# Fetching the K cache in 4 MB units of 32 pairs by 512 keys, with dense score tiles, in a decode attention and MLP kernel

## The chip, the cores and the metric

The kernel runs on one core of a Trainium2 chip, the other cores idle. The metric is the device time of one execution in microseconds (us). A profile is one execution taken with the hardware profiler. Its span (first to last instruction) is about 1.3 us shorter than the measured time.

Engines: PE is TensorE (PEld its weight loads), DVE is VectorE, ACT is ScalarE, POOL is GpSimd, SP is SyncE, whose queue here issues nearly all transfers.

## The reference

The output mixes sliding-window decode attention and a GELU MLP. There are 8 batches, 32 query heads, 16 kv heads of 128, a window of the last 2048 of 8192 keys, and a model width of 576.

```python
g = sigmoid((x * gate_w).sum(-1))
q = (x @ wq).reshape(8, 1, 32, 128)
k, v = last 2048 keys of k_cache, v_cache          # each 8 x 16 pairs of (2048, 128) bf16
p = softmax(q k^T / sqrt(128));  a = (p v) @ wo
b = gelu(layernorm(x) @ w1 + b1) @ w2 + b2
out = g * a + (1 - g) * b
```

The windows of K and V are 67 MB each, the weights 20 MB. Each byte of K and V is used for two query heads only, so this is a memory-bound job. A "pair" below is one batch with one kv head: 512 KB of K in the window, and 2 MiB of the cache, because the cache holds 8192 keys.

## The kernel before

The kernel lists its operations, orders them for each engine when it is built, and emits them with semaphores. Nine slots of 2 MB are shared by K, V and weights, in a ring. K is fetched in 32 units of 2 MB, each 4 batches of one kv head, with each of 128 partitions receiving one contiguous run of 64 keys (16 KB).

```python
def src_of(cache, g, q):
    hkv, b0 = 2 * g + q // 2, 4 * (q % 2)
    return cache[b0:b0 + 4, hkv, S0:Sk, :].rearrange("a (x r) d -> x a (r d)", x=32)

def take_slot():
    n = n_slot[0]; n_slot[0] += 1
    return (n + 6) % NSLOT            # NSLOT = 9, one ring for K, V and weights

def k_unit(i):                        # 32 of them; four make a group g, then softmax(g)
    d = dma("sp", ... slot(s), src_of(A_k_cache, g, q) ..., deps=slot_free[s])
    for h in range(2):
        tr = add("dve", transpose 128x2048 f32 words of the slot -> KT[n % 2], deps=[d, qk_half[n - 2]])
        # first of a group: 4 mask matmuls put -1e9 where query and key belong to different pairs
        # then 8 matmuls, 128 weight columns each (weights held for four), into four PSUM banks
        # PSUM rows: 32 groups' queries x 2048 keys, mostly masked
    slot_free[s] = trs                # the slot goes back after both transposes

def softmax(g):                       # 8 of them
    mx = DVE max over ps[:, 0:4, :]   # 128 x 2048
    ...                               # maximum over the four quadrants, negated and scaled
    for c in range(4): ACT exp of 512 columns, with sum
    for c in range(4): DVE transpose of 512 columns of P -> PT[g % 2]
```

A V unit (2 MB) is multiplied by PT as it lies: 16 matmuls, an eviction by ACT, and 8 small float32 matmuls that add it up. Then the wo projection is added as soon as its head is ready. The order of transfers is K0 to K4, then K and V by turns with four wo chunks between, then b2 and the four w2 chunks, the last of them cut in three.

## Time and profile before

| | before |
|---|---|
| time | 367.79 us (3 runs, 367.7 to 367.86) |
| bytes read | 154.31 MB, 421 GB/s over the span |
| DVE busy, PE busy, ACT busy | 211, 257, 48 us |
| K and V packets | 8192 of 16 KB, 611 ns each |
| tail from the last w2 packet to the end | 2.8 us |

The next lines are from the page of the kernel before. First comes busy time by engine, then the span in 40 slices (busy tenths and GB/s), the bytes, and the shares of the chain that ended last.

```profile
span 366.4 us, 3881 instructions
PE 257.0 (70%) x1815; PEld 86.4 (24%) x1429; DVE 210.7 (57%) x258; ACT 47.8 (13%) x117; POOL 24.3 (7%) x67
DMA  9999999999999999999999999999999999999995
GB/s 378 442 398 427 427 435 432 431 427 431 431 429 429 420 428 427 431 430 433 427 438 431 406 439 429 429 435 427 431 429 429 416 435 435 426 431 433 408 428 224
HBM read 154.31 MB, written 0.01 MB: 421 GB/s over the span
DMA 61%; DVE 17%; PE 16%; SPq 4%; issue 1%; ACT 0%; DVEq 0%
```

The DMA engines are full from the first slice to the last but one, at about 430 GB/s. The chain of waits gives only 61% to DMA, and the rest to DVE and PE. Those pieces are true waits (a slot is handed back by a transpose), but they run beside full DMA engines.

The next lines are groups of instructions before: line, engine, operation, shapes and count, busy time and mean ns, then idle time before it and what ended it. They are the K transpose, the maximum, the exponential and the transpose of P.

```profile
L644 DVE STREAM_TRANSPOSE arena<-arena 128x2048 f32<-128x2048 f32 x64 | 145.4, 2298 | 77.1 <-DMA arena<-in_A_k_cache_dram 64.9
L590 DVE TENSOR_REDUCE arena<-ps 128x1 f32<-128x2048 f32 x8 | 18.3, 2282 | 14.9 <-PE ps L175 14.9
L604 ACT ACTIVATE arena<-ps,arena 128x512 bf16<-128x512 f32 x32 | 21.6, 686 | 39.7 <-DVE arena L599 39.7
L609 DVE STREAM_TRANSPOSE arena<-arena 128x512 bf16<-128x512 bf16 x32 | 19.9, 674 | 0.8 <-ACT arena L604 0.8
```

### The profile page before, as it was taken

The page shows a single profiled execution, that of the slowest core. Times are in us where ns is not written, and L with a number is a line of the kernel's source. Part 1 is how long each engine was busy: PE and PEld are TensorE (multiplying, and loading weights), DVE is VectorE, ACT ScalarE, POOL GpSimd, SP SyncE. Part 2 cuts the span into 40 slices and gives each one's busy share as a digit, 9 for nine tenths or more (in the row PEclk, how much of TensorE's full clock was granted, in tenths as well). Part 3 has the DMA queues.
Part 4 walks back from the last instruction along what each step waited for, and adds up shares of the span by engine and source line. Part 5 has one row for each costly group of instructions (what it writes and reads, how often), then busy time and mean ns, then how long its engine had stood idle before and what let it go on. Part 6 is the DMA issues. An engine that isn't in the chain of part 4 may idle for free.

```text
span 366.4 us, 3881 instructions
## 1 busy us (share of the span) xinstructions
PE 257.0 (70%) x1815; PEld 86.4 (24%) x1429; DVE 210.7 (57%) x258; ACT 47.8 (13%) x117; POOL 24.3 (7%) x67
## 2 busy tenths in 40 slices
PE   0269882896699398664967397765957397865885
PEld 0259200131122032010311032011311032114542
DVE  0704699798667754479544764478544864473000
ACT  1010002101300300013100300003100300003200
POOL 7010000000001000000000000000000000000000
PEclk9999998799689879696988879696988879695659
DMA  9999999999999999999999999999999999999995
GB/s 378 442 398 427 427 435 432 431 427 431 431 429 429 420 428 427 431 430 433 427 438 431 406 439 429 429 435 427 431 429 429 416 435 435 426 431 433 408 428 224
DMA packets 14922, 154.58 MB, mean 422 GB/s; under 512 B 1292, under 2 KB 5556, under 8 KB 6072
## 3 DMA queue, kind: packets, MB, share of 16 engines
q1 hardware_dynamic: 14848, 154.29, 99.2%
q8 instruction: 13, 0.21, 0.2%
q10 hardware_dynamic: 56, 0.03, 0.0%
q14 instruction: 5, 0.04, 0.0%
HBM read 154.31 MB, written 0.01 MB: 421 GB/s over the span
## 4 chain that ended last, share of the span: by engine, by line
DMA 61%; DVE 17%; PE 16%; SPq 4%; issue 1%; ACT 0%; DVEq 0%
DMA arena<-in_A_k_cache_dram 50%; DVE arena L644 12%; DMA arena<-in_B_w_dram 11%; PE ps L175 7%; DVE arena L590 2%; PE ps L501 2%; PE ps L661 2%; PE ps L684 2%; SPq L630 2%; PE ps L699 2%; SPq L677 1%; DVE arena L609 1%; SPq L749 1%; PE ps L503 1%; DVE arena L599 0%
## 5 line engine op out<-in xcount | busy, mean ns | idle before, releaser
L644 DVE STREAM_TRANSPOSE arena<-arena 128x2048 f32<-128x2048 f32 x64 | 145.4, 2298 | 77.1 <-DMA arena<-in_A_k_cache_dram 64.9
L175 PE MATMUL ps<-arena 128*128 128x512 bf16 x401 | 138.1, 456 | 14.7 <-DVE arena L644 9.3
L661 PE MATMUL ps<-arena 128*128 128x512 bf16 x115 | 52.4, 456 | 15.0 <-DVE arena L644 14.9
L693 ACT ACTIVATE arena<-ps 128x512 f32<-128x512 f32 x32 | 19.1, 598 | 198.0 <-PE ps L684 198.0
L661 PEld LDWEIGHTS ps<-arena 128*128 128x128 bf16 x128 | 15.0, 117 | 124.9 <-issue 69.2
L699 PE MATMUL ps<-arena 128*128 128x8 f32 x256 | 35.2, 269 | 8.7 <-ACT arena L693 7.7
L684 PE MATMUL ps<-arena 128*32 128x512 bf16 x512 | 35.6, 403 | 6.7 <-DMA arena<-in_A_v_cache_dram 6.6
L699 PEld LDWEIGHTS ps<-arena 128*128 128x128 f32 x256 | 34.0, 208 | 21.7 <-ACT arena L693 16.8
L653 PE MATMUL ps<-arena 128*128 128x512 bf16 x6 | 3.5, 585 | 36.9 <-DVE arena L609 36.9
L590 DVE TENSOR_REDUCE arena<-ps 128x1 f32<-128x2048 f32 x8 | 18.3, 2282 | 14.9 <-PE ps L175 14.9
L604 ACT ACTIVATE arena<-ps,arena 128x512 bf16<-128x512 f32 x32 | 21.6, 686 | 39.7 <-DVE arena L599 39.7
L637 POOL TENSOR_TENSOR arena<-arena 128x128 bf16<-128x128 bf16 x32 | 12.7, 401 | 165.0 <-PE ps L175 156.2
L684 PEld LDWEIGHTS ps<-arena 128*32 128x32 bf16 x512 | 11.2, 99 | 40.8 <-issue 24.0
L609 DVE STREAM_TRANSPOSE arena<-arena 128x512 bf16<-128x512 bf16 x32 | 19.9, 674 | 0.8 <-ACT arena L604 0.8
L544 PE MATMUL ps<-arena 128*8 128x288 bf16 (+1 forms) x140 | 12.5, 333 | 2.4 <-DMA arena<-in_B_w_dram 2.3
L717 POOL TENSOR_TENSOR arena<-arena 128x16 bf16<-128x16 f32 x15 | 4.0, 267 | 146.3 <-ACT arena L709 146.3
L501 PE MATMUL ps<-arena 128*128 128x8 bf16 x144 | 10.9, 201 | 3.1 <-DMA arena<-in_B_w_dram 3.1
L501 PEld LDWEIGHTS ps<-arena 128*128 128x128 bf16 x144 | 10.8, 158 | 3.6 <-DMA arena<-in_B_w_dram 3.6
L653 PEld LDWEIGHTS ps<-arena 128*128 128x128 bf16 x8 | 0.9, 107 | 44.1 <-DVE arena L609 44.1
L717 DVE TENSOR_TENSOR arena<-ps,arena 128x16 bf16<-128x16 f32 x1 | 0.2, 229 | 18.1 <-PE ps L699 18.1
L423 PE MATMUL ps<-arena 8*128 8x8 bf16 x8 | 0.6, 171 | 13.9 <-DVE arena L396 10.3
L616 DVE RECIPROCAL arena<-ps 128x32 f32<-128x32 f32 x8 | 2.9, 358 | 11.9 <-PE ps L614 11.9
(85 smaller groups left out, 96.3 us busy)
## 6 DMA issues: line engine op xcount, KB each, us to landing
arena<-in_A_k_cache_dram SPq DMA_DIRECT2D x32, 2048.0 KB, 33.7
arena<-in_A_v_cache_dram SPq DMA_DIRECT2D x32, 2048.0 KB, 34.8
arena<-in_B_w_dram SPq DMA_DIRECT2D x1, 4608.0 KB, 23.9
arena<-in_A_wo_dram SPq DMA_DIRECT2D x4, 1152.0 KB, 37.6
arena<-in_A_wq_dram SPq DMA_DIRECT2D x1, 4096.0 KB, 13.6
arena<-in_B_w_dram SPq DMA_DIRECT2D x3, 1296.0 KB, 14.7
arena<-in_B_w_dram SPq DMA_DIRECT2D x3, 576.0 KB, 16.1
arena<-in_A_wq_dram SPq DMA_DIRECT2D x1, 512.0 KB, 4.0
```

The costliest lines, as they stand in the source:

```text
L175: return e.add_instruction(mybir.InstMatmult(name=nc.get_next_instruction_name(), engine=mybir.EngineType.PE, ins=[e.lower_ap(rhs), e.lowe ...
L501: ins = e.matmul(out_, lhsT, yT[:, kt, :], start=(kt == 0), stop=False)
L544: ins = e.matmul(ps[32 * j:32 * j + 8, BK_ACC, 0:JN], lhsT, rhs[:, JN * j:JN * j + JN], start=False, stop=True, skip_group_check=True, til ...
L590: mx = add("dve", lambda e: e.tensor_reduce(out=k(MX), in_=ps[:, 0:4, :].rearrange("p a n -> p (a n)"), axis=AXL.X, op=ALU.max), deps=[qk_ ...
L604: return e.activation(out=Pm[:, 512 * c:512 * c + 512], in_=ps[:, c, :], func=ACTF.Exp, bias=k(NB), scale=SCALE, accum_out=k(SUM + c))
L609: pts.append(add("dve", (lambda c=c: lambda e: e.transpose(bass.AP(arena, offset=aoffs("PT") + 2048 * (g % 2) + 128 * c, ap=[[AST, 128], [ ...
L637: return e.tensor_tensor(out=dst, in0=src, in1=own, op=ALU.mult)
L644: tr = add("dve", (lambda h=h, kb=kb: lambda e: e.transpose(bass.AP(arena_f, offset=foffs("KT") + kb * 2048, ap=[[AST // 2, 128], [1, 2048]]),
L661: mm = e.matmul(*args, start=False, stop=last) if rc == 0 else held_matmul(nc, e, *args, stop=last)
L684: mm = e.matmul(ps[c:c + 32, BK_OS[i % 2], :], PT[:, g % 2, 512 * q + 32 * t:512 * q + 32 * t + 32], slot(s)[:, 512 * t:512 * t + 512], st ...
L693: u_ev[i] = add("act", lambda e: e.activation(out=EV[:, i % 2, :], in_=ps[:, BK_OS[i % 2], :], func=ACTF.Copy), deps=[prev] + ([u_sum[i - ...
L699: mm = e.matmul(ps[:, BK_S, OC + 16 * (item % 2) + 8 * (q % 2):OC + 16 * (item % 2) + 8 * (q % 2) + 8], EV[:, i % 2, 128 * r:128 * r + 128 ...
```

## The change

The intent is to read K in longer runs and to stop computing scores that are thrown away.

- **Transfers.** A K unit becomes 4 MB: 32 neighbouring pairs by 512 keys, and each partition gets a run of 128 keys (32 KB). K has two 4 MB buffers of its own; V has five 2 MB slots.
- **Scores.** Each matmul has 32 weight columns and writes 32 of the 128 PSUM rows, one row block for each K unit of a group, so a bank holds 128 x 512 scores that are all wanted. The mask matmuls go. A softmax now covers one bank: a maximum over 512 columns in place of 2048, and one exponential in place of four. Two softmaxes follow every fourth K unit.
- **Layout of P.** V's matmuls still want the old layout. So the dense tile is copied four times, each time masked to one of four query groups, and transposed from there with a stride.
- **V units.** Still 2 MB and 16 KB runs, but the four pairs of a unit are now eight pairs apart; before, they were one kv head of four batches.
- **End.** A kv head's output is complete only when all four groups are done, so the whole wo projection moves to the end, and so do the wo transfers.

The core of the diff, with cuts:

```diff
+        order = ("0 1 v 2 v 3 v 4 v v 5 v v 6 v v 7 v v 8 v v 9 v v 10 v v 11 v v 12 v v 13 v v 14 v 15 "
+                 "w w v v w w v v v v v v")          # numbers: K units; then b2 and the w2 chunks
         def take_slot():
-            return (n + 6) % NSLOT
+            return 4 + n % 5
         def k_unit(i):
-            d = dma("sp", lambda e: e.dma_start(slot(s), src_of(A_k_cache, g, q)), ...)
+            G, c = divmod(i, 4)
+            s = 2 * (i % 2)
+            src = bass.AP(A_k_cache.tensor, offset=(32 * G * Sk + S0 + 512 * c) * Dh, ap=[[Sk * Dh, 32], [128 * Dh, 4], [1, 128 * Dh]])
+            d = dma("sp", ... RAW[:, s * SE:(s + 2) * SE], src ..., deps=slot_free[s] + slot_free[s + 1])
...  # 8 matmuls for each half and bank:
+            mm = e.matmul(ps[32 * c:32 * c + 32, 2 * (G % 2) + nb, :], qb[:, G % 2, n, 2 * h + ee, :], rhs, ..., tile_position=(0, 32 * c))
         def softmax(g):
-            mx = ... in_=ps[:, 0:4, :] ...
+            mx = ... in_=ps[:, bank, :] ...
-            for c in range(4): activation(out=Pm[:, 512 * c:512 * c + 512], in_=ps[:, c, :], func=ACTF.Exp, ...)
+            ex = activation(out=view("Pd"), in_=ps[:, bank, :], func=ACTF.Exp, ...)
+            for a in range(4): tensor_scalar(out=P[a], in0=Pd, scalar1=amask[:, a:a + 1], op0=ALU.mult)
...
+        def project():                        # called after the last V, before b2
+            for n in range(8):
+                for hkv in (n, n + 8):
+                    AccGroup("proj%d" % hkv, mms, [oT_done[n + 8 * m] for m in range(4)] + [d], cost=0.5)
```

## The prediction

> **What bounds the kernel now.** The transfers. The page shows DMA as 9 in 39 of 40 slices; queue 1 alone takes 99.2% of 16 engines' span, 154.3 MB. In the records of all DMA packets at least 16 are in flight all the time, except for about 2 us at the start and 3.5 us at the end. In the table by stretches every stage from 25 to 345 us runs at 429 to 432 GB/s, while DVE is busy 53 to 76% of a stage and PE 70 to 82%. The chain of waits is 61% DMA; its DVE and PE pieces lie beside full DMA. So compute time saved is worth nothing by itself. The Trainium skill ("DMA: Bandwidth & Descriptors", section "Where 436 GB/s comes from") gives 435 GB/s as the ceiling of the ports; the 431 seen here agrees.
>
> **What the change does to the transfers.** Same bytes. K goes from 16 KB runs to 32 KB runs. In the packet records a 16,384-byte packet takes 611 ns and a 32,768-byte one (wq, median) 1213 ns: 4.5 ns less per 16 KB. K has 4096 such packets, 256 per engine: 1.15 us saved. That is all there is to gain.
>
> **What it does to compute (estimates from the trace's durations).**
> - DVE: 64 K transposes (2.30 us each) become 32 of twice the size, about 4.45 us: 147 to 142 us. The maximum over 2048 columns (8 x 2.28) becomes one over 512 (about 0.65): -13 us. Masked copies: 32 x 0.2 to 0.3: +8 us. The transposes of P (0.67 us) now read with a stride of 512 bytes: 0.7 to 1.4 us: 0 to +22 us. Total 205 to 225 us (211 before), under 62% of the span.
> - ACT: 32 exponentials become 8: -16 us, to about 31 us.
> - PE: 512 score matmuls stay, 32 mask matmuls go; each score matmul loads its own 32-column weights. I expect 0.22 to 0.33 us each, PE 210 to 260 us busy.
>
> None is near the transfer time.
>
> **What moves.** K gets two 4 MB buffers, V five 2 MB slots; before, nine slots were shared. Per 8 MB (K, V, V: 19.5 us at 431 GB/s) DVE has 9 us of transposes, plus some 18 us of softmax each fourth time. A K buffer is handed back 9 to 11 us after landing and needed 25 us or more after. Two places are tight, with 1 to 3 us to spare: K2 at the start (only K1 and one V lie between it and K0, and DVE does the GELU at 38 to 41 us), and the third wo chunk at the end, which waits for the last K's transposes. A stall there costs 0 to 3 us.
>
> **Risk.** The 16 DMA engines now read K side by side at a 2 MiB pitch (one pair each), before at 16 KB. The same page (section "Latency and other measured facts", row "HBM row pitch at large powers of two") reports lower rates at such pitches. No record of this trace shows that pattern, so a fall of the K rate is my main way to lose more than 2%.
>
> **Prediction.** 367.3 us, range 365.6 to 371.5. Faster by over 2%: 0.02; within 2%: 0.87; slower by over 2%: 0.11.
>
> **What would show it.** Right: DMA 9 in nearly all slices at about 430 GB/s; 2048 packets of 32 KB at about 1213 ns; K issues waiting long for DVE without any dip in GB/s; ACT near 31 us. Wrong: 32 KB packets of 1300 ns or more (pitch), GB/s dips at 45 to 55 us or near 310 us (buffers too few), K transposes far above 4.5 us (DVE then becomes the bound), or a tail after the last w2 transfer longer than the 2 to 3 us of before.

## More of the kernel before

The next lines are DMA issues before: out and in, count, KB each, and median us from issue to landing.

```profile
arena<-in_A_k_cache_dram SPq DMA_DIRECT2D x32, 2048.0 KB, 33.7
arena<-in_A_v_cache_dram SPq DMA_DIRECT2D x32, 2048.0 KB, 34.8
```

A transfer of 2 MB moves in 4.9 us at 430 GB/s, so 34 us from issue to landing means that about seven transfers stand in the queue. This is the stock that keeps DMA full while compute is uneven.

The next lines are the end of the kernel before, in order of time on PE: start, duration, instruction, and in brackets the idle time before it and who ended it.

```profile
353.03 6.38 PE L544 MATMUL ps<-arena 128*8 128x288 bf16 x56
360.95 2.03 PE L544 MATMUL ps<-arena 128*8 128x288 bf16 x26 [1.54 <-DMA arena<-in_B_w_dram]
363.71 0.78 PE L544 MATMUL ps<-arena 128*8 128x288 bf16 x10 [0.73 <-DMA arena<-in_B_w_dram]
```

PE waits for w2 twice (1.54 and 0.73 us), so the end is set by the transfer.

## The result

| | before | after |
|---|---|---|
| time, median | 367.83 us (4 runs, 367.7 to 367.97) | 367.9 us (4 runs, 367.75 to 367.98) |
| ratio after / before | | 1.0002, 95% interval 0.9984 to 1.0019 |
| packet time per DMA engine (sum over 16) | 364.66 us | 363.57 us |
| last w2 packet ends at | 363.7 us of 366.4 | 363.1 us of 366.6 |
| tail from there to the end | 2.8 us | 3.5 us |
| DVE, PE, ACT busy | 211, 257, 48 us | 211, 257, 31 us |

Here and below a ratio is the one for the fast runs of both kernels, with its 95% interval; it is not quite the ratio of the medians. The packet rows come from adding up the DMA packet records of the two traces.

These are the same lines of the page after.

```profile
span 366.6 us, 4165 instructions
PE 256.9 (70%) x1805; PEld 131.4 (36%) x1805; DVE 210.9 (58%) x255; ACT 31.0 (8%) x69; POOL 17.5 (5%) x80
DMA  9999999999999999999999999999999999999994
GB/s 374 441 419 431 420 436 445 413 451 402 458 411 442 422 434 434 425 452 406 451 413 447 420 442 422 438 421 434 426 445 422 438 388 440 403 431 431 430 420 187
HBM read 154.31 MB, written 0.01 MB: 421 GB/s over the span
DMA 41%; PE 28%; DVE 28%; issue 1%; SPq 1%; ACT 1%; DVEq 0%
```

DMA is full again, with the same bytes and the same rate. The chain of waits looks quite different (DMA 41% in place of 61%), at the same time to 0.1%. That warns against reading its shares as costs.

These are the groups after: K transpose, maximum, exponential, masked copies and transpose of P.

```profile
L652 DVE STREAM_TRANSPOSE arena<-arena 128x4096 f32<-128x4096 f32 x32 | 141.1, 4432 | 85.3 <-DMA arena<-in_A_k_cache_dram 80.7
L586 DVE TENSOR_REDUCE arena<-ps 128x1 f32<-128x512 f32 x8 | 5.5, 692 | 13.5 <-PE ps L664 13.4
L597 ACT ACTIVATE arena<-ps,arena 128x512 bf16<-128x512 f32 x8 | 5.5, 687 | 115.3 <-DVE arena L595 115.3
L604 DVE TENSOR_SCALAR arena<-arena 128x512 bf16<-128x512 bf16 x32 | 9.0, 345 | 1.0 <-ACT arena L597 0.8
L612 DVE STREAM_TRANSPOSE arena<-arena 128x512 bf16<-128x512 bf16 x32 | 30.6, 1016 | 0.0
```

DVE saves 4 us of K transposes and 13 us of maxima. It pays 9 us for masked copies and 11 us more for the transposes of P. The sum is the same.

The transposes of P now read single 2-byte elements 512 bytes apart, and take 1016 ns in place of 674. The Trainium skill ("SBUF — State Buffer", section "Door 1: The DMA port swizzle") says that SBUF has 16-byte lines and that accesses which cross to a new line pay. The larger duration agrees with that; no run here isolates the stride.

These are the DMA issues after.

```profile
arena<-in_A_k_cache_dram SPq DMA_DIRECT2D x16, 4096.0 KB, 24.9
arena<-in_A_v_cache_dram SPq DMA_DIRECT2D x32, 2048.0 KB, 23.6
```

A transfer now lands 24 us after its issue, not 34. At the same rate this means that less is queued. The time does not show this loss.

This is the end of the kernel after, on PE:

```profile
353.86 1.06 PE L710 MATMUL ps<-arena 128*128 128x8 f32 x8 [0.47 <-ACT arena L704]
357.33 1.06 PE L710 MATMUL ps<-arena 128*128 128x8 f32 x8 [0.46 <-ACT arena L704]
358.31 6.34 PE L544 MATMUL ps<-arena 128*8 128x288 bf16 x96
```

There is no wait for a transfer any more. PE works through 96 projection and w2 matmuls without a gap up to 364.7 us. The w2 data came earlier than before, but PE was behind.

So the trace gives this account of the time. The longer runs save 1.08 us of packet time. The last packet ends 0.5 us earlier. The tail is 0.7 us longer. The last two sum to about zero.

The step from 1.08 to 0.5 us can be read from the same records. Packets that follow each other on an engine overlap a little: the time with more than 16 packets in flight on the main queue, averaged over the 16 engines, adds up to 3.4 us before and 2.8 us after. The sum of packet times counts the overlap twice, so only about 0.5 us of the 1.08 is a shorter transfer.

### The profile page after: what moved, and what is told of

It reads as the page before. It is cut to its first block, busy times and chain, and to the rows that moved or that the text cites. A ratio compares the mean times of both kernels' runs of the same rounds, so it can differ in the third digit from the quotient of the medians.

```text
span 366.6 us, 4165 instructions
## 1 busy us (share of the span) xinstructions
PE 256.9 (70%) x1805; PEld 131.4 (36%) x1805; DVE 210.9 (58%) x255; ACT 31.0 (8%) x69; POOL 17.5 (5%) x80
## 4 chain that ended last, share of the span: by engine, by line
DMA 41%; PE 28%; DVE 28%; issue 1%; SPq 1%; ACT 1%; DVEq 0%
DMA arena<-in_A_k_cache_dram 37%; DVE arena L652 16%; PE ps L664 14%; PE ps L710 8%; DVE arena L612 6%; DMA arena<-in_A_v_cache_dram 4%; PE ps L695 4%; PE ps L544 2%; DVE arena L604 2%; DVE arena L586 1%; DVE arena L595 1%; DVE arena L589 1%; SPq L683 1%; ACT arena L704 1%; DVE arena L618 0%
## 5 line engine op out<-in xcount | busy, mean ns | idle before, releaser
L652 DVE STREAM_TRANSPOSE arena<-arena 128x4096 f32<-128x4096 f32 x32 | 141.1, 4432 | 85.3 <-DMA arena<-in_A_k_cache_dram 80.7
L664 PE MATMUL ps<-arena 128*32 128x512 bf16 x512 | 142.4, 440 | 36.2 <-DVE arena L652 36.1
L664 PEld LDWEIGHTS ps<-arena 128*32 128x32 bf16 x512 | 51.7, 106 | 119.4 <-DVE arena L652 42.2
L695 PE MATMUL ps<-arena 128*32 128x512 bf16 x512 | 56.1, 535 | 32.6 <-DMA arena<-in_A_v_cache_dram 19.6
L695 PEld LDWEIGHTS ps<-arena 128*32 128x32 bf16 x512 | 19.3, 121 | 53.9 <-issue 28.1
L612 DVE STREAM_TRANSPOSE arena<-arena 128x512 bf16<-128x512 bf16 x32 | 30.6, 1016 | 0.0
L731 POOL TENSOR_TENSOR arena<-arena 128x8 bf16<-128x8 f32 x30 | 5.9, 232 | 240.2 <-ACT arena L720 240.2
L597 ACT ACTIVATE arena<-ps,arena 128x512 bf16<-128x512 f32 x8 | 5.5, 687 | 115.3 <-DVE arena L595 115.3
L501 PEld LDWEIGHTS ps<-arena 128*128 128x128 bf16 x144 | 10.8, 157 | 3.1 <-DMA arena<-in_B_w_dram 3.1
L645 POOL TENSOR_TENSOR arena<-arena 128x32 bf16<-128x32 bf16 x32 | 6.5, 241 | 82.0 <-PE ps L664 72.9
L604 DVE TENSOR_SCALAR arena<-arena 128x512 bf16<-128x512 bf16 x32 | 9.0, 345 | 1.0 <-ACT arena L597 0.8
L544 PEld LDWEIGHTS ps<-arena 128*8 128x8 bf16 (+1 forms) x140 | 6.1, 92 | 4.5 <-issue 2.1
```

Of the source, the lines that this page charges most:

```text
L501: ins = e.matmul(out_, lhsT, yT[:, kt, :], start=(kt == 0), stop=False)
L544: ins = e.matmul(ps[32 * j:32 * j + 8, BK_ACC, 0:JN], lhsT, rhs[:, JN * j:JN * j + JN], start=False, stop=True, skip_group_check=True, til ...
L604: return e.tensor_scalar(out=dst, in0=view("Pd").rearrange("p (s n) -> p s n", s=2), scalar1=amask[:, a:a + 1], scalar2=None, op0=ALU.mult)
L612: return e.transpose(dst, src)
L645: return e.tensor_tensor(out=dst, in0=src, in1=own, op=ALU.mult)
L652: tr = add("dve", (lambda h=h, kb=kb: lambda e: e.transpose(bass.AP(arena_f, offset=foffs("KT") + kb * SE // 2, ap=[[AST // 2, 128], [4, 1 ...
```

## The experiments

All are edits of the kernel after, unless they say "before". The ratios are against the kernel before, run on the same chip. The changed kernel was run once more as a yardstick:

> The changed kernel once more, beside the tail experiment on the same chip: 367.9 within 0.2%, 0.0 to 0.2 us from the kernel before.

It measured 368.14 us (367.1 to 368.26), ratio 1.0000 (0.9988 to 1.0012), with a tail of 3.8 us in its profile.

### Does the run length act as costed?

```diff
-            src = ... offset=(32 * G * Sk + S0 + 512 * c) * Dh, ap=[[Sk * Dh, 32], [128 * Dh, 4], [1, 128 * Dh]]
+            for hh in range(2):       # two transfers on the same semaphore
+                src = ... offset=(32 * G * Sk + S0 + 512 * c + 64 * hh) * Dh, ap=[[Sk * Dh, 32], [128 * Dh, 4], [1, 64 * Dh]]
```

> The changed kernel, each 4 MB K unit fetched as two transfers with 16 KB runs instead of one with 32 KB runs; everything else the same. Transfer theory: 4096 packets of 611 ns in place of 2048 of 1213 ns, packet time per engine up by 1.1 us (363.6 to 364.7), the last transfer lands about 0.6 to 1.1 us later; the span grows by 0 to 0.6 us, because the end of the changed kernel waits for TensorE and has some slack. Rival, the longer runs brought nothing or the larger unit matters: packet time unchanged.

The packet time per engine was 364.74 us, against 363.57 and 363.39 in the two profiles of the changed kernel: 1.2 to 1.4 us more. The last w2 packet ended at 363.9 us in place of 363.1 and 363.0. The time was 368.76 us (367.81 to 371.26), ratio 1.0031 (1.0007 to 1.0054). So the packet time moved as costed. The transfer itself changed less: here too the overlap of packets is 3.4 us in place of 2.8. The last packet came 0.8 to 1.0 us later. By the medians the time rose by 0.6 to 0.9 us, at or above the upper end of what was expected; the interval is wide.

### Does the engine pitch in HBM matter?

Partitions are filled in groups of four with one pair's runs, and the pairs lie 2 MiB apart. This edit makes it 8 MiB, on other data.

```diff
-offset=(32 * G * Sk + S0 + 512 * c) * Dh, ap=[[Sk * Dh, 32], ...
+offset=(G * Sk + S0 + 512 * c) * Dh, ap=[[4 * Sk * Dh, 32], ...
```

> The changed kernel, but a K unit takes every fourth pair instead of 32 neighbours: the runs that the 16 engines read side by side lie 8 MiB apart instead of 2 MiB. Wrong result on purpose. If pitch does not matter to a pure load: 32 KB packets stay at 1213 ns and the time within 0.3%. If the fall that the Trainium skill tabulates for large pitches holds for loads: packets of 1500 ns or more and 40 us or more on top.

The time was 378.62 us (376.25 to 380.2), ratio 1.0289 (1.0254 to 1.0324). That is neither of the two forecasts. (The row they refer to is in "DMA: Bandwidth & Descriptors", section "Latency and other measured facts"; its figures stand near the end of this text.) The result is wrong by construction, but the comparison with the reference did not notice it at its tolerance. The same holds for the other wrong kernels below, so "correct" proves little in this problem.

The mean time of the 128 packets of each K unit, from the packet records, tells more. The last row is the time from the first start to the last end of a unit, less the time of its eight packets: a measure of how far the 16 engines have drifted apart.

| mean packet start in the unit (us), 8 MiB | 30 | 58 | 74 | 110 | 130 | 150 | 209 | 287 |
|---|---|---|---|---|---|---|---|---|
| packet, 8 MiB pitch (ns) | 1489 | 1421 | 1345 | 1331 | 1316 | 1213 | 1217 | 1213 |
| packet, same unit in the changed kernel, 2 MiB (ns) | 1217 | 1218 | 1213 | 1213 | 1213 | 1213 | 1216 | 1216 |
| drift, 8 MiB pitch (us) | 1.0 | 2.0 | 2.5 | 3.1 | 3.3 | 4.3 | 4.3 | 5.2 |

At 8 MiB the first K unit was 23% slow (1489 over 1213). The loss shrank, though not evenly (two units that are not in the table, at 42 and 90 us, had 1408 and 1277 ns), and was gone when the engines were about 4 us apart. Stretches of the same run, and below them of the changed kernel, show it too. The columns are the stretch, busy time by engine, granted clock, DMA share and GB/s.

```profile
25.00:60.00 35.00, 24.70 (x233) 16.09 (x234) 19.03 (x9) 1.06 (x3) 3.20 (x16) 1.00 1.02 379
60.00:150.00 90.00, 59.40 (x335) 26.73 (x333) 59.37 (x56) 6.07 (x14) 2.79 (x14) 0.83 1.00 410
150.00:280.00 130.00, 87.51 (x548) 42.08 (x546) 86.64 (x102) 12.31 (x29) 4.34 (x22) 0.82 1.00 430
```

```profile
25.00:60.00 35.00, 28.04 (x244) 17.19 (x244) 19.72 (x10) 1.15 (x3) 3.21 (x16) 1.00 1.00 431
60.00:150.00 90.00, 65.01 (x356) 29.54 (x356) 59.92 (x55) 6.85 (x16) 2.80 (x14) 0.81 1.00 431
```

Note that the DMA share is full in both. A busy DMA engine may be a slow one, so GB/s has to be read beside it. The pitch is a real risk, and at the change's own 2 MiB it cost next to nothing (1215 ns on average against 1213). That engines in step hinder each other at 8 MiB is a reading that fits the drift; no run forced them apart to prove it.

### Is compute really free?

The first theory was that only transfers count. The rival took the chain of waits at its word. The edit does the first half-unit's transpose twice, for K units 2 to 13:

```diff
                 tr_hist.append(tr)
+                if h == 0 and 2 <= i <= 13:
+                    tr = add("dve", <the same transpose again>, deps=deps + [tr], name="trx...", after=tr_hist[-1:])
+                    tr_hist.append(tr)
```

> The changed kernel, with the first K transpose of K units 2 to 13 done twice: 12 x 4.43 = 53 us more VectorE work between about 60 and 300 us, same result. Transfer theory: time within 0.3% of the changed kernel (367.9), DVE busy 264 us, no dip in GB/s, waits of K issues for DVE shorter or at other places. Rival, the chain of waits taken at its word (28% DVE, 28% PE, 41% DMA): DVE pieces are on the path, so 15 to 53 us more.

The time was 382.8 us (379.38 to 384.62), ratio 1.0385 (1.0341 to 1.0430): 15 us more for 53 us of added work, at the edge of what the rival expected. The transfer theory in its simple form is refuted. The page shows holes in the transfers:

```profile
DMA  9999999999997999999999999999989499999994
GB/s 383 422 423 427 428 444 439 415 456 407 449 377 260 416 452 413 442 423 437 425 418 396 416 437 417 446 423 444 415 325 411 200 350 416 396 436 432 434 421 196
```

Two costs can be read from the packet records. The 16 engines stood idle for about 12 us between 100 and 320 us, where the changed kernel had no idle time. And the packets took 3.9 us longer per engine (367.50 against 363.57). Of that, 2.5 us lie in four K units, each just after a hole: K6, K10, K14 and K15 averaged 1258 to 1315 ns per packet. There it is nearly all in the first packet of each engine: in K6 the first took 2038 ns, the second to eighth 1211 to 1213. So a hole costs its own length and, by the excess over 1213 ns in these four units, 0.4 to 0.8 us more to start again. It is not the pitch effect, which was spread over all packets of a unit.

Is there a threshold? Half the dose, on the changed kernel and on the kernel before:

```diff
+                if h == 0 and i in (2, 4, 6, 8, 10, 12):       # changed kernel, 6 x 4.43 us
+                if h == 0 and 4 <= i <= 27 and i % 2 == 0:     # kernel before, 12 x 2.31 us
```

> The changed kernel with six first-half K transposes (K units 2, 4, 6, 8, 10, 12) done twice: 6 x 4.43 = 27 us more VectorE work, half of the dose of the earlier run. Floor theory: the cut kernel's 306 us plus 27 stays below 366, so the time does not move. Queue theory: what counts is how much is still queued when the next transfer is issued (K6: 6.2 us, K4 and K14: 9 us in the changed kernel); a delay of 4.4 us at a time uses that up at one or two units: 1 to 6 us longer, with short dips in GB/s.

> The kernel before with twelve first-half K transposes (every second K unit from 4 to 26) done twice: 12 x 2.31 = 28 us more VectorE work, the same dose. Queue theory: before, 28 us of transfers are queued at the median issue and 5.5 us at the lowest, and 2.3 us at a time are less: time within 0.3%, less than the changed kernel loses. Floor theory: the cut kernel's 324 plus 28 stays below 366: no change either. If the kernel before loses as much as the changed one, its longer queue buys nothing.

The changed kernel took 368.14 us (367.35 to 370.99), ratio 1.0021 (0.9987 to 1.0055). The kernel before took 367.91 us, ratio 1.0005 (0.9990 to 1.0021). DVE was busy 237 us in both, 26 to 27 us more than without the edit. The 1 to 6 us that were expected for the changed kernel did not show: its interval reaches from 0.5 us less to 2.0 us more. So 27 us of DVE work fit into its slack, to within about 2 us, and 53 us do not. Its slowest run (370.99) hints that it is near the edge, but the profile is of its fastest run (367.35), and one run is no proof.

What is used up is the stock of queued transfers. It can be computed at each issue: the bytes issued earlier, less the bytes moved by then (packet records), over 430.8 GB/s. The moment taken is the end of the issuing instruction, and a packet counts as moved when it has ended. This matters where issuing itself takes long: K13 of the kernel before took 18 us to issue and had 23 us of work ahead of it when it began; why, the trace does not say. These are microseconds of queued work ahead of some transfers:

| transfer | before | changed | changed, +27 us DVE | changed, +53 us DVE |
|---|---|---|---|---|
| median, all K, V and wo transfers after 26 us | 27.9 | 14.9 | 13.7 | 9.7 |
| lowest of them | 5.5 (K13) | 3.5 (V26) | 3.0 (K6) | 0.0 (K6, K15) |
| K2 of the changed kernel | | 3.7 | 3.8 | 3.7 |
| K6 of the changed kernel | | 6.2 | 3.0 | 0.0 |
| K14 of the changed kernel | | 9.4 | 5.2 | 0.1 |

In the first three columns no entry falls below 3.0 us, and the time does not move. In the last column K6, K14 and K15 reach zero, and the time goes. The edge lies somewhat above zero: in the same run V5 and K10 were issued with 1.7 and 1.0 us ahead of them and still left the engines idle for 0.4 and 0.5 us, while the first wo chunk with 2.5 us left no hole. (K6 of the third column, at 3.0 us, left 0.1 us.) The change halved the median stock and paid nothing for it, because all that counts is that it does not run out.

Why is K6 low? It takes K4's buffer, which is free when both of K4's transposes are done. The DVE timeline of the changed kernel around it (the transposes at 97.04 and 106.83 are K4's):

```profile
89.36 0.69 DVE L586 TENSOR_REDUCE arena<-ps 128x1 f32<-128x512 f32 x1
91.81 3.79 DVE L612 STREAM_TRANSPOSE arena<-arena 128x512 bf16<-128x512 bf16 x4
97.04 4.45 DVE L652 STREAM_TRANSPOSE arena<-arena 128x4096 f32<-128x4096 f32 x1
102.58 3.87 DVE L612 STREAM_TRANSPOSE arena<-arena 128x512 bf16<-128x512 bf16 x4
106.83 8.76 DVE L652 STREAM_TRANSPOSE arena<-arena 128x4096 f32<-128x4096 f32 x2
```

K4's last packet ended at 89.5 us. Its first transpose waited for the first softmax, its second stood behind the second softmax, and the buffer was free at 111.2 us (K6 was issued at 111.29): 22 us, not 9 to 11. The same count for the other K units gives 18 us for K8 and K12, 14 us for K5, and 9 to 10 us for the remaining twelve: it is the unit behind each fourth one that meets the softmaxes.

### How many V slots?

```diff
-            return 4 + n % 5
+            return 4 + n % 3          # and, in another kernel, n % 4
```

> The changed kernel with three V slots instead of five. The V that needs the new softmax holds its slot until about 22 us after the fourth K unit landed; with five slots the next V is needed about 39 us after, with three about 20 us after. Transfer theory: the SP queue now stands still two to four times for 3 to 8 us each with GB/s dips after each fourth K unit: 10 to 30 us longer. Rival (buffers have much slack): no change.

> The changed kernel with four V slots instead of five. With three the SP queue stood still at V3, V11, V19 and lost 25 us; with four the V that waits for the new softmax is V4, V12, V20, one V or one K unit later in the stream. Queue theory: nothing to 6 us longer, with the queue empty or nearly so at those three. If five slots are needed with no margin: 10 us or more.

With three slots it took 394.81 us (392.55 to 395.65), ratio 1.0725. With four it took 380.61 us (377.86 to 381.21), ratio 1.0331. With this order of transfers five slots are thus needed. With three, the expected 10 to 30 us came (27). With four, the queue stood at exactly the named V4, V12 and V20 (0.0, 0.0 and 0.3 us of stock), but the cost was twice the most that was expected (12.7 us in place of 0 to 6). The engines were idle for 6.1, 2.3 and 1.4 us there; packets took 1.5 us more per engine (365.07), and the tail was 1.4 us longer (4.8). The DMA rows of the page with four slots:

```profile
DMA  9999999997599999997999999998999999999994
GB/s 389 422 416 437 425 457 425 417 435 338 221 440 431 454 404 454 409 444 311 420 432 444 414 456 407 433 434 350 426 449 420 430 392 440 397 435 430 426 383 143
```

### What lies under the transfers?

Both kernels with every K and V transfer after a buffer's first fill cut to a quarter (compute unchanged, stale data):

```diff
+            fr = 1 if i < 2 else 4                       # changed kernel, K; i < 5 for V; before: the first nine transfers
-ap=[..., [1, 128 * Dh]]) ... RAW[:, s * SE:(s + 2) * SE]
+ap=[..., [1, 128 * Dh // fr]]) ... RAW[:, s * SE:s * SE + 2 * SE // fr]
```

> The changed kernel, but every K and V transfer after the first fill of its buffer brings only a quarter of its bytes (runs of 8 KB for K, 4 KB for V); all compute as before, on stale data. Wrong result on purpose. About 67 MB in place of 154 MB, 156 us at 431 GB/s. It shows the floor that compute sets under the transfers: DVE 211 us plus its unfilled waits. I expect 250 to 290 us, less than the same cut of the kernel before. If compute mattered to the time of the whole kernel, the fall would be much smaller (above 340 us).

> The kernel before with the same cut: after each buffer's first fill, a quarter of the bytes of each K and V transfer. Wrong result on purpose. Its scores of one group fill all four banks that the next group needs, so softmax and scores cannot overlap: I expect 270 to 310 us, 10 to 30 us more than the changed kernel with the cut. If the change brings compute nothing at all: equal.

The changed kernel took 305.94 us (303.45 to 307.9), and the kernel before 323.78 us (322.2 to 326.32). Both are 14 to 16 us above the ranges expected, so the floors are higher than I had worked out; their difference, 18 us, is as expected. The bytes and the chains of waits, changed kernel first:

```profile
DVE 42%; PE 41%; DMA 11%; issue 2%; ACT 2%; SPq 0%; DVEq 0%
HBM read 67.80 MB, written 0.01 MB: 221 GB/s over the span
```

```profile
PE 64%; DVE 23%; DMA 8%; ACT 2%; issue 1%; SPq 0%; DVEq 0%
HBM read 67.80 MB, written 0.01 MB: 211 GB/s over the span
```

The same bytes were read, and DMA is no longer the chain. So the compute of the changed kernel as a whole is 18 us faster, although in these two runs DVE is busy equally long (211 us) and PE only 5.5 us less (234.8 against 240.3). The rest must lie in waits; I take it to be the banks, which now alternate between groups, but no run isolates that from the new order of transfers and the moved projection. It lies 62 us and 44 us below the 368 us that the transfers set, and so it cannot be seen.

### Does the end eat the saving?

First try: fetch the last two K units earlier, so that PE's backlog starts earlier. The softmax calls were also deferred in the build, to keep the dependences valid.

```diff
-... 11 v v 12 v v 13 v v 14 v 15 " "w w v v w w v v v v v v"
+... 11 v v 12 v 13 v 14 v 15 " "w w v v w w v v v v v v v v"
```

> The changed kernel with its last two K units fetched earlier, ahead of two V units (12 v 13 v 14 v 15 in place of 12 v v 13 v v 14 v 15), so that the last softmax and the backlog of TensorE behind it begin about 10 us sooner. Same result. The end of the changed kernel is a TensorE backlog from 331 to 364.7 us; if that ate the 1.1 us of shorter packet time, the tail after the last w2 packet falls from 3.5 to 2.7 us and the time by 0.5 to 0.8 us against the changed kernel; else nothing changes.

It took 370.71 us (369.98 to 373.51), ratio 1.0086 (1.0063 to 1.0109): slower. The stock explains it in part. With a V less between the K units, K14 was issued with 0.6 us of stock and K15 with 2.1 (9.4 and 13.0 in the changed kernel). The engines idled 1.1 us, packets took 0.7 to 0.9 us more, and the last w2 packet ended at 364.9 us. The tail was 4.5 us, not shorter. Two more V units now came after the last K, and the last 88 matmuls took 8.28 us, where the 96 of the changed kernel took 6.34. The run tested two things at once and does not decide the question.

Second try: drop the projection of eight of the sixteen kv heads, and nothing else.

```diff
-            for n in range(8):
+            for n in range(4):
                 for hkv in (n, n + 8):
```

> The changed kernel without the projection of eight of the sixteen kv heads: 32 of the matmuls with 288 columns fall away from the TensorE backlog at the end, about 2 us. Wrong result on purpose. If that backlog sets the end: time 0.6 to 1.0 us less than the changed kernel (368.0), the tail after the last w2 packet 2.7 to 2.9 us in place of 3.5 to 3.8. If the transfers set it: unchanged.

It took 367.16 us (367.02 to 367.19, 5 runs), ratio 0.9979 (0.9967 to 0.9992), which is 1.0 us below the yardstick's median and 0.8 us by the ratios. The tail was 2.8 us, as in the kernel before, and PE waits for w2 again:

```profile
356.15 6.72 PE L544 MATMUL ps<-arena 128*8 128x288 bf16 x62
363.21 0.78 PE L544 MATMUL ps<-arena 128*8 128x288 bf16 x10 [0.34 <-DMA arena<-in_B_w_dram]
```

The last w2 packet ended at 363.15 us, as in the changed kernel, so the whole difference is the tail, 0.7 to 1.0 us in the profiles. The times alone are less sharp: the two intervals overlap at their edges, and one of the yardstick's runs took 367.1 us. So the backlog on PE at the end, which the late projection makes, costs the changed kernel about as much as the longer runs brought the last packet forward (0.5 to 0.7 us).

## Why the prediction was right, and where it was not

- **"The transfers" bound the kernel; no gain from compute.** Right. DMA was full before and after, and the 17 us less on ACT and 18 us of a lower compute floor left no mark. The sentence "compute time saved is worth nothing by itself" held. Its mirror image does not: the 53 us dose cost 15 us.
- **"1.15 us saved. That is all there is to gain."** Right as a sum of packet times: the records show 1.08 us, and undoing the run length alone gave 1.2 to 1.4 us back. But packets overlap, and the last one came only 0.5 to 0.7 us earlier, so the step from packet time to transfer time was too large, by up to a factor of two.
- **DVE 205 to 225 us, ACT about 31, PE 210 to 260.** Right: 211, 31 and 257. The K transposes took 4.43 us (4.45 expected), the maximum 0.69 (0.65), the transposes of P 1.02 (0.7 to 1.4). A masked copy took 0.345 us where 0.2 to 0.3 was expected, but four in a row overlap, and their 9 us of busy time was close to the 8 expected.
- **"A K buffer is handed back 9 to 11 us after landing and needed 25 us or more after."** Half wrong. K4 took 22 us, because the two softmaxes stand between its transposes on DVE, and three other units took 14 to 18 us. The prediction named K2 (3.7 us of stock) and the third wo chunk (4.9 us) as tight, rightly, and missed K6 (6.2 us) and V26 (3.5 us). None came near zero, so it cost nothing. The late hand-back is where the 53 us dose hurt first: K6, K10 and K14, which take the buffers of K4, K8 and K12, are three of the four units behind holes.
- **Tail of "2 to 3 us".** It was 3.5 to 3.8 us. The prediction listed a longer tail as a sign of error but had no term for it, although the projection visibly moved to the end. That term is 0.7 to 1.0 us and cancels the saving: measured 367.9 instead of 367.3. The range of 365.6 to 371.5 us is wide enough to hold either way, so it is no evidence that these small terms were right.
- **Pitch as the main risk.** The pattern does slow loads down, at 8 MiB by 11 us in all, but at the change's 2 MiB packets took 1215 ns against 1213. The Trainium skill ("DMA: Bandwidth & Descriptors", section "Latency and other measured facts") gives 207 GB/s at 512 KiB, 164 at 2 MiB and 103 at 8 MiB, for copies between HBM tensors. This load agreed in direction only: 379 against 431 GB/s in its worst stretch at 8 MiB, and under 0.5% of packet time at 2 MiB.

No version here beats either kernel by a margin that matters. With the same bytes, and DMA full for all but about 4 us, what these runs show as left to win on one core is the 0.5 to 1 us of run length and about 1 us of tail.

## What to carry to other kernels

When DMA is at nine in every slice at the full rate, cost a change first by its packets (count times duration) and then by the two ends, where transfers and compute do not overlap; ignore the rest. "Off the critical path" is not "free to grow": work out how many microseconds of transfers are queued at each issue, because compute may take about that much more before the queue runs dry (here holes worth counting began at about 2 us, not at zero). Test a buffer count by taking one away: five slots were silent here and four cost 13 us.

## What the Trainium skill lacked or had wrong

- "DMA: Bandwidth & Descriptors", "Latency and other measured facts", row on the HBM row pitch: it has copies between HBM tensors only, and calls the loss "Independent of how many tiles are touched". In loads from HBM to SBUF at 8 MiB the loss was 23% in the first K unit and zero from the eighth on, as the engines drifted about 4 us apart; at 2 MiB it was under 0.5%.
- The same page, "Where 436 GB/s comes from", gives 435 GB/s as the fabric ceiling. The full stretches here ran at 429 to 432 GB/s, and one of the changed kernel (60 to 120 us) at 435. Its remark that for HBM to SBUF "the HBM side (~358) binds" did not hold with one core running; the remark leaves out what the page says further up, that this figure is for two cores streaming.
- The same page has no durations of large packets. Here: 1152 bytes 51 ns, 10,368 bytes 389 ns, 16 KB 611 ns, 32 KB 1213 ns, 36 KB 1364 ns. Doubling 16 KB runs is worth 0.7% of their packet time.
- No page that I read says how much must be queued ahead on a DMA queue. Here a stock of 3.0 us at the lowest issue was enough (0.1 us of idle). Issues at 1.7 and 1.0 us left the engines idle for 0.4 and 0.5 us, and issues at 0.0 for 2 to 11 us, depending on how late they came; in the 53 us run the first 32 KB packet of each engine after a hole took up to 2038 ns on average instead of 1213.
- "SBUF — State Buffer" has the 16-byte lines but no duration for the DVE transpose read with a stride: 1016 ns for 128x512 bf16 at a stride of 512 bytes, 674 ns with a contiguous source.
